# Moving cos and sin from k to v in a fused cosine attention and token mixer, with one transpose of q per head pair, whole-tile stores and a new instruction order

## Chip, cores, metric

One core of one Trainium2 chip. The metric is device microseconds of one execution. The profile's span is about 1.8 us shorter than the time (128.5 against 130.29 us for the profiled run before); spans are compared with spans and times with times. Executions of one kernel differ: a run over 1.5% above the fastest of the same kernel is marked slow, and only fast runs are compared. Clock is the mean share of TensorE's full clock that was granted; "half clock" is a stretch at 0.5.

## The reference, cut

```python
def _attn_ref(q, k, v):                      # 8 batches, 8 heads, 576 tokens, 64 dims
    theta = np.pi / 2.0 * np.arange(S) / S
    def phi(x, c, s):                        # features: relu(x) * cos, relu(x) * sin
        r = np.maximum(x, 0.0)
        return np.concatenate([r * c, r * s], axis=-1)
    q_p, k_p = phi(q, cos_w, sin_w), phi(k, cos_w, sin_w)
    kv = np.einsum('bhsf,bhsd->bhfd', k_p, v)
    z = np.sum(k_p, axis=2)
    num = np.einsum('bhsf,bhfd->bhsd', q_p, kv)
    den = np.einsum('bhsf,bhf->bhs', q_p, z)[..., None] + 1e-06
    return num / den

def _moe_ref(x, w_q, w_k, w_out):            # x: heads side by side, 576 x 512 per batch
    W_tok = (1.0 / np.sqrt(64)) * np.einsum('bsd,btd->bst', x @ w_q, x @ w_k)
    mixed = np.einsum('bst,btd->bsd', W_tok, x)
    return np.maximum(mixed, 0.0) @ w_out
```

The kernel uses that there is no softmax: k'v is 128 features by 64 per head, and the mixer takes (x w_k)' x, which is 64 by 512 per batch.

## The kernel before

An explicit list, `ORDER`, gives every operation, its indices and its engine (`T` TensorE with a bank number, `V` VectorE, `A` ScalarE, `G` GpSimd, `Y` SyncE). Each engine runs its own in order. A head's 576 tokens lie as 64 rows of 9 tokens (`C9`), so two heads stack on 128 partitions, and `H` counts units of four heads (two pairs). The steps of one pair: load (`LD`), relu of k (`RK`), product with cos and sin (`MK`), relu of q, written twice side by side (`DQ`), cast of v (`CV`), k'v and q transposes (`QK`), evacuations of both, that is, copies out of TensorE's output banks (`EK`, `EQ`), num (`NM`), reciprocal (`RC`), scaling (`XN`, the tile `xs`). The mixer: transposes of x (`XT`, `EX`), its products (`WQK`, `TK`, `KX`, `MX`) with evacuations, the output projection (`WO`), output copy (`EO`), store (`ST`).

```python
    def QK(eng, pb, g):                       # per head hh: k'v, then q transposed twice over
        H, i = divmod(g, 2)
        qt, kvp = qk_views(pb)
        for c in range(C9):
            for hh in range(2):
                p0 = hh * 64
                T.matmul(kvp[:, hh, :], kp[H % N_KP][p0:p0 + 64, i, c, :, :],
                         vb[H % N_VB][p0:p0 + 64, i, c, 0:D + 1], start=(c == 0), stop=(c == C9 - 1))
        # ... q transposes of 64 rows, out of the doubled qd
    def EK(eng, pb, g):
        copy(eng, kvs[g % N_KV], qk_views(at["QK", g])[1])

    # MX multiplies for a run of chunks of columns, (0, 5) or (5, 9): mix stays in the order
    # (c, d), so a 128-row output tile holds two runs of 64 tokens, 9 tokens apart
    def ST(eng, pb, b, u, hi):                # one store for each half (hi) of a tile
        ts = (UNITS7 if b == B - 1 else UNITS[b % 2])[u]
        n, _ = unit_of[b, ts[0]]
        bl, c = divmod(2 * (ts[0] + 4 * (b % 2)) + hi, C9)
        row = ((b // 2) * 2 + bl) * S + c
        dst = dataclasses.replace(out, offset=out.offset + row * DM,
            ap=[[C9 * DM, 64], [2 * DM, len(ts)], [1, DM]])
        eng.dma_start(dst, osb[n % N_OSB][64 * hi:64 * hi + 64, 0:len(ts), :])
```

The end of `ORDER`, where 42 stores are shared by two queues, SyncE's (30) and ScalarE's own (12):

```
WO.7.2@T7 ST.6.1.1@A EO.7.1@V WO.7.4@T0 EO.7.2@A WO.7.3@T1 ST.7.1.0@Y ST.7.1.1@A EO.7.4@V
WO.7.0@T2 ST.7.3.0@A EO.7.3@V ST.7.3.1@A ST.7.2.0@Y EO.7.0@A ST.7.2.1@Y ST.7.0.0@A ST.7.0.1@Y
```

## Time and profile before

| | before |
|---|---|
| time, median of 3 (range) | 130.89 us (130.32 to 133.51) |
| span of the profile, clock | 128.5 us, 0.91 |
| last load issued | 99.9 us |
| last of the 32 `xs` scalings ends | 108.6 us |
| last output copy ends | 124.1 us |

The prediction prints the main lines. Three more views matter for what came out. The first is the chain that ended last, its last pieces (start, length, what):

```profile
117.78 2.71 PE banks L413 x12
...
120.51 0.70 DVE osb L187
...
121.23 0.54 ACTq L430
...
121.81 1.60 ACTq L430
...
123.51 0.58 ACT osb L185
```

`ACTq L430` is ScalarE's sequencer issuing stores. It is not counted as busy, but the last output copy, `ACT osb`, is behind it in the same queue: two issues, 2.1 us, on the chain.

The second is the store line looked at by itself: duration of one issue in ns (min/median/max), then first and last start in us.

```profile
L430 SPq DMA_DIRECT2D out_dram<-osb x30: 466/607/1414, 64.6 to 124.1; - x30
...
L430 ACTq DMA_DIRECT2D out_dram<-osb x12: 498/616/1596, 73.8 to 124.1; - x12
```

The third is SyncE's timeline (start, length, what) where the last load is issued:

```profile
94.61 5.25 SPq L430 DMA_DIRECT2D out_dram<-osb  x2
99.91 0.60 SPq L208 DMA_DIRECT2D vf<-in_v_dram  x1
```

Two stores, the second of which waited for an output tile, stand directly ahead of the last load.

### The profile page before, as it was taken

The page shows a single profiled execution, that of the slowest core. Times are in us where ns is not written, and L with a number is a line of the kernel's source. Part 1 is how long each engine was busy: PE and PEld are TensorE (multiplying, and loading weights), DVE is VectorE, ACT ScalarE, POOL GpSimd, SP SyncE. Part 2 cuts the span into 40 slices and gives each one's busy share as a digit, 9 for nine tenths or more (in the row PEclk, how much of TensorE's full clock was granted, in tenths as well). Part 3 has the DMA queues.
Part 4 walks back from the last instruction along what each step waited for, and adds up shares of the span by engine and source line. Part 5 has one row for each costly group of instructions (what it writes and reads, how often), then busy time and mean ns, then how long its engine had stood idle before and what let it go on. Part 6 is the DMA issues. An engine that isn't in the chain of part 4 may idle for free.

```text
span 128.5 us, 5197 instructions
## 1 busy us (share of the span) xinstructions
PE 105.4 (82%) x2198; PEld 69.4 (54%) x2198; DVE 106.2 (83%) x227; ACT 77.5 (60%) x124; POOL 69.4 (54%) x81
## 2 busy tenths in 40 slices
PE   5935594887879979878999969889999999999900
PEld 2314584847667546566676557364576775543400
DVE  3466999987899999999999896999999998774600
ACT  7125443966396698974976758647977655147110
POOL 7009817098969979995078252389949740020000
PEclk9995558655799999999999999999999999999995
DMA  4999999999999999992068999999998799468793
GB/s 133 276 389 406 391 391 390 331 392 388 389 387 392 391 385 391 390 386 103 5 146 319 303 360 363 340 329 403 384 377 309 176 341 248 107 197 278 186 289 100
DMA packets 20711, 39.40 MB, mean 307 GB/s; under 512 B 3280, under 2 KB 3280, under 8 KB 20688
## 3 DMA queue, kind: packets, MB, share of 16 engines
q1 hardware_dynamic: 19152, 36.32, 81.8%
q10 hardware_dynamic: 1536, 2.75, 6.1%
q8 instruction: 17, 0.28, 0.9%
q14 instruction: 6, 0.05, 0.1%
HBM read 29.62 MB, written 9.44 MB: 304 GB/s over the span
## 4 chain that ended last, share of the span: by engine, by line
DVE 31%; PE 30%; POOL 10%; DMA 8%; SPq 7%; issue 6%; ACT 3%; ACTq 2%; POOLq 0%
DVE kp L232 10%; PE banks L413 10%; DVE xs L309 8%; DVE qpt L279 7%; POOL qd L195 5%; PE banks L260 5%; SPq L208 5%; DMA qf<-in_q_dram 5%; PE banks L269 4%; DMA vf<-in_v_dram 4%; PE banks L292 3%; SPq L430 2%; DVE rec L305 2%; PE banks L343 2%; POOL vb L189 2%
## 5 line engine op out<-in xcount | busy, mean ns | idle before, releaser
L195 POOL TENSOR_SCALAR qd<-qf 128x1152 bf16<-128x1152 f32 x32 | 39.1, 1231 | 12.7 <-DMA qf<-in_q_dram 11.6
L413 PE MATMUL banks<-wo_sb,mix 128*128 128x512 bf16 x144 | 36.0, 380 | 0.0
L232 DVE TENSOR_TENSOR kp<-rk,cossin 128x1152 bf16<-128x1152 bf16 x32 | 29.2, 932 | 1.4 <-POOL rk L195 1.3
L185 ACT COPY osb<-banks 128x512 f32<-128x512 f32 x31 | 18.0, 589 | 12.9 <-PE banks L413 8.2
L309 DVE TENSOR_TENSOR xs<-banks,rec 128x640 bf16<-128x640 f32 x32 | 25.4, 808 | 0.3
L279 DVE TENSOR_TENSOR qpt<-banks,cst 128x1152 bf16<-128x1152 bf16 x32 | 23.9, 746 | 1.1 <-PE banks L269 0.8
L401 ACT ACTIVATE mix<-banks 128x640 bf16<-128x640 f32 (+1 forms) x27 | 17.4, 656 | 8.7 <-PE banks L388 8.1
L260 PE MATMUL banks<-vb,kp 64*128 64x65 bf16 x576 | 16.7, 202 | 3.8 <-DVE kp L232 1.8
L413 PEld LDWEIGHTS <-mix 128*128 128x128 bf16 x144 | 12.1, 98 | 12.5 <-issue 1.4
L292 PE MATMUL banks<-kvs,qpt 128*128 128x65 bf16 x320 | 16.2, 203 | 3.1 <-DVE kvs L187 2.2
L269 PE MATMUL banks<-ident,qd 64*128 64x64 bf16 x576 | 16.2, 201 | 2.2 <-POOL qd L195 2.2
L292 PEld LDWEIGHTS <-qpt 128*128 128x128 bf16 x320 | 13.8, 103 | 7.1 <-DVE qpt L279 2.5
L260 PEld LDWEIGHTS <-kp 64*128 64x128 bf16 x576 | 13.6, 100 | 7.2 <-DVE kp L232 2.5
L193 ACT ACTIVATE rk<-kf 128x576 bf16<-128x576 f32 x15 | 10.1, 684 | 9.1 <-DMA kf<-in_k_dram 8.9
L195 POOL TENSOR_SCALAR rk<-kf 128x576 bf16<-128x576 f32 x14 | 11.3, 812 | 6.6 <-DMA kf<-in_k_dram 2.8
L189 POOL TENSOR_SCALAR vb<-vf 128x576 bf16<-128x576 f32 x17 | 12.3, 726 | 4.6 <-DMA vf<-in_v_dram 3.5
L269 PEld LDWEIGHTS <-qd 64*128 64x128 bf16 x576 | 12.9, 102 | 2.4 <-POOL qd L195 2.4
L185 ACT COPY xT<-banks 128x1280 bf16<-128x1280 bf16 x10 | 12.2, 1225 | 2.9 <-PE banks L326 2.9
L185 ACT CAST vb<-vf 128x576 bf16<-128x576 f32 x14 | 9.4, 673 | 4.7 <-DMA vf<-in_v_dram 4.5
L326 PE MATMUL banks<-ident,xs 64*128 64x64 bf16 x320 | 7.8, 196 | 4.2 <-DVE xs L309 4.1
L189 POOL TENSOR_SCALAR wq<-wqk 64x576 bf16<-64x576 bf16 x4 | 2.8, 712 | 14.9 <-DVE wqk L187 7.8
L343 PE MATMUL banks<-xT,wqk_sb 128*128 128x288 bf16 x64 | 10.1, 306 | 0.7 <-DVE xs L309 0.3
(46 smaller groups left out, 112.8 us busy)
## 6 DMA issues: line engine op xcount, KB each, us to landing
kf<-in_k_dram SPq DMA_DIRECT2D x32, 288.0 KB, 6.0
vf<-in_v_dram SPq DMA_DIRECT2D x32, 288.0 KB, 5.9
qf<-in_q_dram SPq DMA_DIRECT2D x32, 288.0 KB, 6.0
out_dram<-osb SPq DMA_DIRECT2D x21, 256.0 KB, 4.4
out_dram<-osb ACTq DMA_DIRECT2D x9, 256.0 KB, 4.3
out_dram<-osb SPq DMA_DIRECT2D x9, 128.0 KB, 3.4
wo_f<-in_moe_w_out_dram SPq DMA_DIRECT2D x1, 1024.0 KB, 8.3
out_dram<-osb ACTq DMA_DIRECT2D x3, 128.0 KB, 4.0
```

The lines of the kernel that those rows point to most:

```text
L185: A.copy(dst, src)
L189: eng.tensor_scalar(dst, src, 1.0, 1.0, op0=ALU.mult, op1=ALU.mult)
L195: eng.tensor_scalar(dst, src, FMAX, 0.0, op0=ALU.min, op1=ALU.max)
L232: eng.tensor_mul(kp[H % N_KP][:, lo:hi], rk[H % N_RK][:, lo:hi].unsqueeze(3).to_broadcast([P, n, C9, 2, D]), cossin.unsqueeze(1).to_broadc ...
L260: T.matmul(kvp[:, hh, :], kp[H % N_KP][p0:p0 + 64, i, c, :, :], vb[H % N_VB][p0:p0 + 64, i, c, 0:D + 1], start=(c == 0), stop=(c == C9 - 1))
L269: T.transpose(qt[:, hh, c * D:(c + 1) * D], src, ident[p0:p0 + 64, p0:p0 + 64])
L279: eng.tensor_mul(qpt[g % N_QPT][:, :, 1:SLOTS, :], qk_views(at["QK", g])[0].rearrange("f h (c d) -> f h c d", c=C9), cst.unsqueeze(1).to_b ...
L292: T.matmul(nv[:, hh, u, :], qpt[g % N_QPT][:, hh, 2 * u:2 * u + 2, :], kvs[g % N_KV][:, hh, :], start=(u == 0), stop=(u == SC - 1 and not ...
L309: eng.tensor_tensor(xs[b % N_XS][:, :, 2 * pr:2 * pr + 2, :].rearrange("p u h d -> p h u d"), num_view(at["NM", g])[:, :, :, 0:D], rec[g % ...
L343: T.matmul(w[:, nh, :], wqk_sb[:, dmc, :], xT[b % N_XT][:, dmc, D + nh * HS:D + (nh + 1) * HS], start=(dmc == 0), stop=(dmc == NDM - 1))
L401: A.activation(dst, src, AF.Relu, scale=scale_moe)
L413: T.matmul(o, mix[b // 2 % N_MIX][:, dmc, base:base + P], wo_sb[:, dmc, :], start=(dmc == 0), stop=(dmc == NDM - 1))
```

## The change

The intent: take work off VectorE, the busiest engine, and make fewer, larger instructions.

1. cos and sin go into v instead of k (`VK`, with a column of cos or sin to give the denominator). k'v is then a 64-row by 64-column product, and four run side by side in quarters of the array.
2. q is no longer written twice. Its transpose is made once per two heads stacked in rows, and `EQ` reads it for cos and for sin.
3. One ScalarE copy evacuates k'v of four heads (262 columns), in place of two VectorE ones of 130.
4. x is transposed in full 128x128 tiles (`XT_FULL`).
5. `MX` takes strided columns and `EMX` writes mix in token order, so an output tile is 128 consecutive tokens and goes out in one store: 21 stores on SyncE.
6. A new `ORDER`, which also moves evacuations from VectorE to ScalarE, k relus to GpSimd, and all stores to SyncE. The numbers of buffers change with it, among them the output tiles (6 to 8).

```diff
-            eng.tensor_mul(kp[...], rk[...].unsqueeze(3).to_broadcast([P, n, C9, 2, D]), cossin...)
+    def VK(eng, pb, H, j):
+        eng.tensor_mul(vv[H % N_VV][:, j, :, :, 0:D],
+            vb[H % N_VB][:, j].unsqueeze(2).to_broadcast([P, C9, 2, D]), cossin)
...
+    def KV(eng, pb, H):
+        kvp = bank2(pb, 0, 4 * NV, FP32)
+        for c in range(C9):
+            for j in range(2):
+                for r in range(2):
+                    T.matmul(kvp[64 * j:64 * j + 64, r, :], rk[H % N_RK][64 * r:64 * r + 64, j, c, :],
+                             vv[H % N_VV][64 * r:64 * r + 64, j, c].rearrange("p w d -> p (w d)")[:, 0:NV],
+                             start=(c == 0), stop=(c == C9 - 1))
...
     def NM(eng, pb, g):
-        for hh in range(2):
-            for u in range(SC):
-                T.matmul(nv[:, hh, u, :], qpt[g % N_QPT][:, hh, 2 * u:2 * u + 2, :],
-                         kvs[g % N_KV][:, hh, :], ...)
+        for u in range(SC):
+            for w in range(2):
+                for j in range(2):
+                    p0 = 64 * j
+                    T.matmul(nv[:, j, u, :], qpt[g % N_QPT][p0:p0 + 64, w, 2 * u:2 * u + 2, :],
+                             kvs[H % N_KV][p0:p0 + 64, r, w, 0:D + 1], ...)
...
     def XT(eng, pb, H):
+                if full:
+                    T.transpose(xv[:, i, u, :], x, ident)
+                    continue
...
     def MX(eng, pb, b, j):
-        c0, c1 = ((0, 5), (5, 9))[nh]
+                     w.rearrange("p (c d) -> p c d", c=C9)[:, :, h * TH:(h + 1) * TH],
     def EMX(eng, pb, b, j):
+            :, :, i, o:o + NT].rearrange("p r (d c) -> p r d c", c=C9)
...
-    def ST(eng, pb, b, u, hi):
-            ap=[[C9 * DM, 64], [2 * DM, len(ts)], [1, DM]])
-        eng.dma_start(dst, osb[n % N_OSB][64 * hi:64 * hi + 64, 0:len(ts), :])
+    def ST(eng, pb, b, u):
+        row = (b // 2) * 2 * S + (ts[0] + 4 * (b % 2)) * P
+            out, offset=out.offset + row * DM, ap=[[DM, P], [P * DM, len(ts)], [1, DM]])
+        eng.dma_start(dst, osb[n % N_OSB][:, 0:len(ts), :])
```

## The prediction

> **What bounds the kernel now.** I read the page first, then the busy time by stretches, the waits of the SP queue, and the groups by form.
>
> The page, engines and slices:
>
> ```profile
> PE 105.4 (82%) x2198; PEld 69.4 (54%) x2198; DVE 106.2 (83%) x227; ACT 77.5 (60%) x124; POOL 69.4 (54%) x81
> ...
> DVE  3466999987899999999999896999999998774600
> ...
> PEclk9995558655799999999999999999999999999995
> DMA  4999999999999999992068999999998799468793
> ```
>
> DVE is at 9 from 18 us to about 105 us. DMA is full up to 57 us, has a hole at 60 to 67 us, and is full again to 93 us. PE runs at half clock for about 20 us in the first 34 us.
>
> The stretches (length, then PE, PEld, DVE, ACT, POOL busy, clock, DMA share, GB/s):
>
> ```profile
> 36.00:60.00 24.00, 20.91 (x526) 14.16 (x525) 23.55 (x48) 18.87 (x31) 21.37 (x22) 1.00 0.99 367
> 60.00:68.00 8.00, 7.83 (x210) 5.67 (x203) 7.90 (x18) 6.50 (x11) 3.00 (x3) 1.00 0.29 64
> 68.00:100.00 32.00, 29.44 (x687) 19.40 (x686) 29.79 (x66) 22.77 (x38) 20.25 (x23) 1.00 0.98 350
> ...
> 100.00:128.50 28.50, 21.89 (x288) 11.90 (x283) 17.05 (x33) 10.71 (x19) 3.97 (x6) 0.95 0.74 216
> ```
>
> From 36 to 100 us DVE works 61.2 of 64 us, 96%. PE shows 91%, but that counts each matmul's latency: a 128x65 num matmul lasts 203 ns and starts every 29 to 34 ns, so PE has more room than it shows. The DMA hole is an effect of slow compute:
>
> ```profile
> SPq L208 <- ACT rk L193: 8.6, 1, 8.6
> ```
>
> One load of k waits 8.6 us for a raw buffer, because the relu that frees it stands behind a late ACT queue. The last load is issued at 99.9 us. The work before it is DVE-bound; the 28.6 us after it are a tail of mixer work, in which PE is full from 110 to 120 us.
>
> The groups that the change touches:
>
> ```profile
> L195 POOL TENSOR_SCALAR qd<-qf 128x1152 bf16<-128x1152 f32 x32 | 39.1, 1231 | 12.7 <-DMA qf<-in_q_dram 11.6 <-PE banks L269 0.3
> L232 DVE TENSOR_TENSOR kp<-rk,cossin 128x1152 bf16<-128x1152 bf16 x32 | 29.2, 932 | 1.4 <-POOL rk L195 1.3
> L279 DVE TENSOR_TENSOR qpt<-banks,cst 128x1152 bf16<-128x1152 bf16 x32 | 23.9, 746 | 1.1 <-PE banks L269 0.8
> L185 ACT COPY osb<-banks 128x512 f32<-128x512 f32 x31 | 18.0, 589 | 12.9 <-PE banks L413 8.2 <-issue 3.3 <-DMA qf<-in_q_dram 0.9
> L187 DVE CAST kvs<-banks 128x130 bf16<-128x130 f32 x32 | 8.7, 281 | 1.1 <-ACT xT L185 1.0
> L187 DVE COPY xT<-banks 128x1280 bf16<-128x1280 bf16 x6 | 4.8, 815 | 0.0
> L187 DVE COPY osb<-banks 128x512 f32<-128x512 f32 x5 | 3.5, 692 | 2.8 <-PE banks L413 2.8
> ```
>
> **What the Trainium skill says.** (1) "SBUF — State Buffer", Who interferes with whom: a Vector tensor_tensor with both inputs in SBUF contends with GpSimd for an exclusive port pair. The trace agrees: the 13 kp products with under 20% of their time beside POOL average 0.68 us, the 12 with over 80% average 1.07 us. (2) "VectorE: DVE Perf Modes", Why PSUM operands drop a tier: a PSUM operand still allows the 2x bf16 mode, fp32 stays at 1x. It agrees: qpt from PSUM takes 0.746 us for 1152 elements, about the 0.75 us median of kp, so the new broadcast form should too. (3) "TensorEngine Tiling (Array Packing)", Key Properties: a change of tiling mode drains TensorE, and tiles run independently. It agrees: a 512-column matmul is followed by the same mode after 216 ns, by another after 312 ns, so a drain is about 0.1 us. (4) The same page, Gotcha 2: column tiling excludes fast weight load. The trace fits: the 64-column weight loads of kx take 110 ns, the 128-column ones 95 to 98 ns; two column tiles still load 3 to 4 ns apart, so four 64x64 tiles should overlap. The trace before has no 64x64 tiles, so that step is inferred.
>
> **The change, part by part.** Durations are the group means. The two programs' engine queues give the counts.
>
> DVE. The k product becomes the v product (cos and sin go into v): 32 products of 1152 elements either way, 29.2 us or a little less, as POOL has less work. The q product (32 x 0.746), num scaling (32 x 0.81) and reciprocals stay. Removed: 32 kvs casts, 8.7; five output copies, 3.5; three of six xT copies, 2.4; four of five mix relus, 2.9; three k relus, 1.7; one v cast, one wqk, two kx copies, 2.4; one more wkj copy costs 0.3. Sum -21.3 us. 106.2 becomes about 85.
>
> ACT. Added: 16 kvs copies of 262 columns at about 0.375 (kx of 256 takes 0.370), 6.0; 14 q relus at 0.68, 9.6; five output copies, 2.9; three xT copies, 3.7; four mix relus, 2.6; kx, wqk and cst, 1.9. Removed: eight k relus, 5.5; two v casts, 1.3; three wq copies, 2.0; one wkj, 0.4. Sum +17.5: 77.5 becomes about 95. ACT's 12 store issues go to SP, some 0.6 us each that were never counted as busy, so ACT's real load rises by about 10.
>
> POOL. 32 q relus of 1152 elements (39.1) become 18 of 576 at about 0.75 (13.5), since q is no longer duplicated. Added: 11 k relus at 0.81, 8.9; three v casts, 2.2; three wq copies, 2.1; six small copies of cos, about 1. Sum -11: 69.4 becomes about 58.
>
> PE, at full clock, from start-to-start times in the trace. k'v: 32 x 0.285 = 9.1 before; after, 16 x 9 groups of four tiles, 131 columns at 2.4 columns/ns = 55 ns, with 0.05 for fill: 16 x 0.55 = 8.8. q transposes: 32 x 0.26 = 8.3, then 16 x 0.26 = 4.2. num: 32 x 0.31 = 9.9, then 32 x 20 x 14.5 ns = 9.3. xs transposes: 16 x 0.29 = 4.6, then full tiles 160 x 56 ns = 9.0. Mode changes, counted from the order: 80 to 97, +1.7 us. The output projection (36 x 0.86 = 31) and the mixer stay. Sum: -0.3 -4.1 -0.6 +4.4 +1.7 = about +1. PE is neutral at about 90 us.
>
> DMA. The same 39.4 MB, at the 390 GB/s of the full slices 101 us. 42 stores of 64 rows become 21 of 128, so SP has 119 issues and ACT none. Eight output buffers instead of six allow stores to come late: only six stand ahead of the last load, 14 or more before.
>
> **The sum.** I cut the time at the last load's issue. Before: DVE has about 88 us of work ahead of it; start at 8 us plus 88/0.96 gives 99.7, measured 99.9. After: work ahead of it, total minus the operations listed after it, is DVE 85-15 = 70, ACT 95-24 = 71, PE 90-28 = 62 plus some 10 for half clock; DMA 29.6 MB plus 2.6 of stores less 2 in flight, 30.2/0.39 = 77. With starts at 8, 4, 5 and 2 us the floors are 78, 75, 77 and 79: four resources nearly level. No resource is then at 96% as DVE was; I allow 8 us for waits in turn, so 87 us. The tail: 28 us of PE work remain (19 output tiles alone 16.3, before only 14), ACT 24, and the last copy and store need 2 to 3: about 31, against 28.6. Span 118; the measured time before is about 2 us over its profile span: 120. I choose 119.5.
>
> **The rivals.** *ACT becomes the bound.* It evacuates kvs, xT, wqk, kx, mix and every output tile in one in-order queue, and now also holds kvs on the way from k'v to num. For it: the 8.6 us wait above shows one late ACT instruction stopping loads. Against: 95 of 118 us is 80%. If ACT loses a further 6 us, the time is about 126. *Column tiling serializes.* If the 64x64 weight loads go one after another at 27 ns (an estimate: the 13 ns by which kx loads exceed the fast ones is half of a 64-column load at 2.4 columns/ns), each k'v takes 0.97 us, PE gains 7 us, and the end is about 123. Against: the 3 ns start distance of kx pairs. *DMA hides the gain.* If stores pile up at the end, 15 stores of at most 0.5 MB stand after the last load, under 7 MB, 18 us in 31: not a bound unless bunched, +2 us. *Better than balanced:* if loads stay full to the last, the end is near 112 to 114.
>
> **Range and chances.** DVE's 21 us are real removals from the binding engine, and no floor is over 80 us up to the last load, so slower needs two rivals at once. Range 113.5 to 126. Faster by over 2% (under 128.3) 0.88, within 2% 0.09, slower 0.03.
>
> **What would show it.** DVE busy 82 to 88 us with the v product at 0.7 to 0.95 us; ACT 92 to 98; POOL 55 to 62; k'v about 0.55 us per 36 matmuls at full clock; no DMA hole over 3 us before the last load; last load issued at 83 to 91 us; tail 29 to 33 us. It is wrong if the v product falls out of the 2x mode (over 1.2 us each, +15 us of DVE), if the transposed read of the mix copies slows them from about 0.65 us (31 on ACT; 0.2 us more each is +6 us), if PE's half clock lasts beyond 40 us, or if stores on SP hold up loads.

## The result, and the profile after

After: median 123.97 us (123.52 to 125.53), before in the same session 130.92 us. The ratio is 0.9472, with an interval of 0.9417 to 0.9527. A ratio is the mean time of one kernel's fast runs over that of the other's fast runs of the same rounds, so not quite the ratio of the medians quoted. One run after (125.53) was slow and is not used; the profile: span 122.0, clock 0.93.

The page after, engines and slices:

```profile
PE 104.4 (86%) x2056; PEld 67.0 (55%) x2070; DVE 87.2 (71%) x174; ACT 92.0 (75%) x155; POOL 58.7 (48%) x90
...
PE   5934885999686999998969997999999999999970
...
DVE  2054899859999798999999995987798779412000
...
DMA  4999999999999999998996299999999896244595
```

VectorE lost 19 us of work and is at 9 in fewer slices. PE stands at 9 from the slice at 76 us to 116 us. There is still a gap in DMA at 64 to 70 us.

The stretches after (length, then PE, PEld, DVE, ACT, POOL busy, clock, DMA share, GB/s):

```profile
36.00:60.00 24.00, 21.98 (x493) 13.82 (x495) 22.26 (x41) 20.43 (x37) 18.55 (x23) 1.00 1.00 359
60.00:68.00 8.00, 6.92 (x178) 5.06 (x179) 7.64 (x17) 7.62 (x13) 3.30 (x4) 1.00 0.77 276
68.00:100.00 32.00, 30.69 (x669) 20.02 (x673) 26.88 (x53) 26.69 (x49) 17.36 (x24) 1.00 0.96 350
100.00:122.00 22.00, 17.95 (x184) 9.30 (x186) 5.67 (x14) 14.14 (x25) 1.33 (x2) 1.00 0.57 211
```

Before, VectorE was busy 29.79 of the 32 us from 68 us; now it is 26.88, and PE is the highest with 30.69. The groups that answer to those of before:

```profile
L219 DVE TENSOR_TENSOR vv<-vb,cossin 128x1152 bf16<-128x1152 bf16 x32 | 27.8, 893 | 7.1 <-ACT vb L180 6.1
L257 DVE TENSOR_TENSOR qpt<-banks,cst 128x1152 bf16<-128x1152 bf16 x32 | 22.9, 747 | 4.5 <-PE banks L250 4.2
...
L180 ACT COPY osb<-banks 128x512 f32<-128x512 f32 x36 | 20.9, 591 | 2.4 <-PE banks L403 1.7
...
L190 POOL TENSOR_SCALAR qd<-qf 128x576 bf16<-128x576 f32 x18 | 13.4, 745 | 14.6 <-DMA qf<-in_q_dram 13.9
...
L180 ACT CAST kvs<-banks 128x262 bf16<-128x262 f32 x16 | 6.1, 381 | 6.5 <-PE banks L236 6.3
```

Each of these operations costs about what was foreseen. VectorE now idles (7.1 us in front of `vv`) for casts of v on ScalarE. The wait of SyncE behind the DMA gap (us in total, times, longest) is one v cast on ScalarE, where before it was a k relu on ScalarE:

```profile
SPq L197 <- ACT vb L180: 5.6, 1, 5.6
```

The end of the chain after, and the store line:

```profile
113.03 4.64 PE banks L403 x21
...
117.72 0.61 PE banks L403 x2
...
118.36 0.59 ACT osb L180
```

```profile
L418 SPq DMA_DIRECT2D out_dram<-osb x21: 332/394/2037, 59.1 to 119.0; - x21
```

The last copy now starts when its matmuls end (0.04 us after them); before, it started 1.3 us after them. That is half of what was gained behind the last matmul. Most of the other half is the last store itself: from issue to landing it took 3.3 us before and takes 2.2 now. A store of 128 rows holds its queue for 0.39 us in the median, one of 64 rows held it for 0.61. Summed, issuing stores takes 10.5 us of SyncE; before it took 22.2 us of SyncE and 8.3 us of ScalarE.

**Where the 6.5 us of span went.** Both kernels make 32 scalings `xs` of the same shape, so the trace can be cut at the end of the ninth, of the last, and at the end of the last matmul. The table holds all kernels, from their profiles. The last column is the state of that profile; rows marked slow are for reading only. Each figure is rounded by itself.

| kernel | start to 9th scaling | 9th to last | to last matmul | to the end | span | state |
|---|---|---|---|---|---|---|
| before | 42.9 | 65.7 | 13.6 | 6.3 | 128.5 | fast |
| after | 39.3 | 65.1 | 13.9 | 3.7 | 122.0 | fast |
| e3_before_newmix | 41.7 | 65.8 | 13.6 | 3.7 | 124.8 | fast |
| e1_ek_dve | 38.9 | 65.6 | 13.9 | 3.7 | 122.1 | fast |
| e3_dve_heavy | 44.3 | 73.8 | 13.9 | 3.7 | 135.6 | fast |
| e2_xt_twice | 40.2 | 68.8 | 15.0 | 3.7 | 127.7 | fast |
| e1_cv_pool | 36.6 | 66.1 | 13.9 | 3.7 | 120.4 | fast |
| e2_warm | 37.4 | 65.9 | 13.9 | 3.7 | 121.0 | fast |
| e3_best | 38.5 | 64.6 | 13.9 | 3.7 | 120.8 | fast |
| e1_old_mix | 36.7 | 68.9 | 14.0 | 6.7 | 126.3 | slow |
| e2_store_split | 38.9 | 67.7 | 14.4 | 6.5 | 127.4 | slow |
| e2_before_act | 43.0 | 69.8 | 14.0 | 6.6 | 133.4 | slow |
| e1_xt_half | 39.9 | 65.8 | 13.8 | 3.7 | 123.2 | slow |
| e3_best_half | 40.8 | 64.6 | 13.8 | 3.7 | 122.9 | slow |

From before to after: -3.6, -0.6, +0.3, -2.6. VectorE's busy time in these stretches went from 34.8 to 28.1 us, from 62.5 to 57.3 and from 8.9 to 1.9. So only 5.2 of its 19 us went out of the long middle, where it was 95% busy, and that stretch hardly got shorter.

### The profile page after: what moved, and what is told of

It is laid out like the page before. It is cut to its first block, busy times and chain, and to the rows that moved or that the text cites. A ratio compares the mean times of both kernels' runs of the same rounds, so it can differ in the third digit from the quotient of the medians.

```text
span 122.0 us, 4895 instructions
## 1 busy us (share of the span) xinstructions
PE 104.4 (86%) x2056; PEld 67.0 (55%) x2070; DVE 87.2 (71%) x174; ACT 92.0 (75%) x155; POOL 58.7 (48%) x90
## 4 chain that ended last, share of the span: by engine, by line
PE 49%; DVE 26%; DMA 15%; issue 4%; ACT 2%; SPq 1%; POOL 1%; ACTq 0%; DVEq 0%
PE banks L403 20%; DVE vv L219 10%; DVE xs L292 7%; DVE qpt L257 6%; DMA qf<-in_q_dram 6%; PE banks L236 5%; PE banks L332 5%; DMA kf<-in_k_dram 5%; PE banks L271 5%; PE banks L379 4%; DMA vf<-in_v_dram 4%; PE banks L360 3%; PE banks L310 3%; PE banks L250 2%; DVE rec L287 2%
## 5 line engine op out<-in xcount | busy, mean ns | idle before, releaser
L219 DVE TENSOR_TENSOR vv<-vb,cossin 128x1152 bf16<-128x1152 bf16 x32 | 27.8, 893 | 7.1 <-ACT vb L180 6.1
L391 ACT ACTIVATE mix<-banks 128x576 bf16<-128x576 f32 x31 | 19.5, 655 | 2.3 <-PE banks L379 1.0
L190 POOL TENSOR_SCALAR qd<-qf 128x576 bf16<-128x576 f32 x18 | 13.4, 745 | 14.6 <-DMA qf<-in_q_dram 13.9
L271 PE MATMUL banks<-kvs,qpt 64*128 64x65 bf16 x640 | 15.3, 198 | 1.0 <-ACT kvs L180 0.9
L271 PEld LDWEIGHTS <-qpt 64*128 64x128 bf16 x640 | 13.1, 99 | 4.6 <-issue 2.7
L236 PE MATMUL banks<-vv,rk 64*64 64x131 bf16 x576 | 14.3, 237 | 1.4 <-DVE vv L219 0.6
L236 PEld LDWEIGHTS <-rk 64*64 64x64 bf16 x576 | 10.8, 116 | 4.6 <-issue 2.9
L188 ACT ACTIVATE qd<-qf 128x576 bf16<-128x576 f32 x14 | 9.6, 686 | 4.2 <-DMA qf<-in_q_dram 4.0
L310 PE MATMUL banks<-ident,xs 128*128 128x128 bf16 x160 | 12.3, 231 | 0.0
L310 PEld LDWEIGHTS <-xs 128*128 128x128 bf16 x160 | 10.3, 104 | 2.3 <-DVE xs L292 0.3
```

The costliest lines, as they stand in the source:

```text
L190: eng.tensor_scalar(dst, src, FMAX, 0.0, op0=ALU.min, op1=ALU.max)
L219: eng.tensor_mul(vv[H % N_VV][:, j, :, :, 0:D], vb[H % N_VB][:, j].unsqueeze(2).to_broadcast([P, C9, 2, D]), cossin)
L236: T.matmul(kvp[64 * j:64 * j + 64, r, :], rk[H % N_RK][64 * r:64 * r + 64, j, c, :], vv[H % N_VV][64 * r:64 * r + 64, j, c].rearrange("p w ...
L271: T.matmul(nv[:, j, u, :], qpt[g % N_QPT][p0:p0 + 64, w, 2 * u:2 * u + 2, :], kvs[H % N_KV][p0:p0 + 64, r, w, 0:D + 1], start=(u == 0 and ...
L310: T.transpose(xv[:, i, u, :], x, ident)
L391: A.activation(dst, src, AF.Relu, scale=scale_moe)
```

## The experiments

Three theories stood at the outset: the gain comes from VectorE's relief and its balance with ScalarE; TensorE has become the limit of the second half; loads, and the gap in DMA, set the end. The rival to all three: the form of the stores (halves or whole tiles) does it. Every kernel here gave the right result. "Before" was run again with each set; its medians there were 132.02, 132.09 and 131.97 us, with 17 of those 25 runs slow, so the ratios have wide intervals. Where it helps, the text compares fast runs with fast runs of "after" (mean of three, 123.82). "After" was not run again with the sets, and the third set (e3) ran on another chip than the first two; the mean of the fast runs of "before" moved between 130.06 and 131.35 us from set to set. So differences to "after" of about 1 us are not told from noise.

### Stores

**e1_old_mix**: the mixer products, mix and stores of before, in the new order.

```diff
-                     w.rearrange("p (c d) -> p c d", c=C9)[:, :, h * TH:(h + 1) * TH],
+            w = (wqk[b % N_WQK][0:64, D + c0 * D:D + c1 * D] if r == 0 else wq2[...])
-        eng.dma_start(dst, osb[n % N_OSB][:, 0:len(ts), :])
+        for hi in range(2):
+            ST1(eng, pb, b, u, hi)          # 64 rows, 9 tokens apart, as before
```

> The changed kernel, with mix, its relu copies and the stores as in the kernel before (chunks of 5 and 4 columns of 64, stores of 64 rows each, two for one, all on SP: 42 instead of 21). Theories 1 to 3 all expect the same time within 1 us, since the copies cost the same 0.655 us on average and the stores are not the bound. The rival that whole-tile stores carry part of the gain expects 2 to 4 us slower, with loads held up behind stores on SP.

Measured: median 127.17 us, ratio 0.9736 (0.9549 to 0.9923). The fast runs, 125.76, 127.0 and 127.34, average 2.9 us over the fast runs of after. So undoing only this part loses about two fifths of the gain: the rival is right here. The profile was slow; its last column in the table, 6.7 us, is taken up below.

**e2_store_split**: is it the order of mix or the store's form? Token order stays, each store goes out as two of 64 rows.

```diff
-        eng.dma_start(dst, osb[n % N_OSB][:, 0:len(ts), :])
+        for hi in range(2):
+            dh = dataclasses.replace(out, offset=out.offset + (row + 64 * hi) * DM,
+                                     ap=[[DM, 64], [P * DM, len(ts)], [1, DM]])
+            eng.dma_start(dh, osb[n % N_OSB][64 * hi:64 * hi + 64, 0:len(ts), :])
```

> The changed kernel, with each store of 128 rows issued as two of 64 rows, both on SP, mix still in token order: 42 stores instead of 21. The run with the old mix and the old stores was 3 us slower; its last output copy ended 1.3 us later than in the changed kernel, but its end 4.3 us later. If the number of stores on SP does that: 2 to 4 us slower than the changed kernel, the last store issued about 2.5 us or more after the last output copy. If the old row order of mix does it: within 1 us.

Measured: 127.35 us, ratio 0.9691 (0.9598 to 0.9784); fast runs 127.14, 127.22 and 127.49, 3.5 us over after. The form of the store alone gives all that e1_old_mix gave. Its store line, as above:

```profile
L421 SPq DMA_DIRECT2D out_dram<-osb x42: 487/610/1878, 59.1 to 124.0; - x42
```

610 ns for 64 consecutive rows, 607 for 64 rows that lie 9 apart: their spacing makes no difference here, and 128 rows took 394. These are medians; single issues lasted up to 1.9 us here and 2.0 us in after. SyncE's timeline from 112 us to the end, of after and then of the split:

```profile
112.01 7.29 SPq L418 DMA_DIRECT2D out_dram<-osb  x6
```

```profile
112.10 12.49 SPq L421 DMA_DIRECT2D out_dram<-osb  x14
```

The lengths run from the first start to the last end, waits for output tiles included. With whole tiles the last store starts 0.03 us after the last copy (118.94 us). With halves, eight issues stand almost without a gap from 118.86 us on, and four of them start after the last copy (121.54 us), the last at 124.0. That is the end column: 6.3 to 6.7 us from the last matmul to the end in each of the four kernels with half-tile stores, 3.7 in each of the ten with whole tiles, whatever else they do, in fast and slow profiles alike.

**e3_before_newmix**: the same part put alone into the kernel before. The two halves of mix take 36 and 28 of the 64 rows, since with 32 and 32 an output tile of the old order would read columns not yet written. There are 14 stores on SyncE and 7 on ScalarE.

```diff
-        c0, c1 = ((0, 5), (5, 9))[nh]
+        d0, d1 = ((0, 36), (36, 64))[h]
+                     w.rearrange("p (c d) -> p c d", c=C9)[:, :, d0:d1],
-            ap=[[C9 * DM, 64], [2 * DM, len(ts)], [1, DM]])
+            ap=[[DM, P], [P * DM, len(ts)], [1, DM]])
-WO.7.0@T2 ST.7.3.0@A EO.7.3@V ST.7.3.1@A ST.7.2.0@Y EO.7.0@A ST.7.2.1@Y ST.7.0.0@A ST.7.0.1@Y
+WO.7.0@T2  EO.7.3@V ST.7.3@A  EO.7.0@A ST.7.2@Y  ST.7.0@Y
```

> The kernel before, with only the mix in token order (halves of 36 and 28 of the 64 steps, so that its own order of operations stays valid) and stores of whole tiles: 21 instead of 42 issues, each at the place of the second of its pair, on the queue of that one. Splitting the stores in the changed kernel cost 3.3 us. If that part of the gain stands alone: 2 to 4 us faster than before. If it is only worth something with the new order (because before, ScalarE's queue took 12 of the stores): within 1 us of before.

Measured: 126.24 us, six fast runs from 126.03 to 126.81; ratio 0.9711 (0.9611 to 0.9811), against only two fast runs of before. About 3.7 us gained by the fast means (126.34 against 130.06), and all six runs are below all eleven of before. No work was taken off any engine:

```profile
PE 105.3 (84%) x2198; PEld 69.0 (55%) x2198; DVE 106.8 (86%) x227; ACT 77.9 (62%) x124; POOL 70.3 (56%) x81
```

VectorE is as busy as before, and the middle took 65.8 us as before. Of the 3.7 us of span, 2.6 lie behind the last matmul. Here the chain ends as in after: no `ACTq` stands before the last copy, although ScalarE still issues seven stores.

```profile
116.60 4.44 PE banks L414 x20
...
121.06 0.59 ACT osb L185
```

The other 1.2 us lie before the ninth scaling at 41.7 us, while the first store is issued at 64.6: no store can have made them. Half clock lasted 17.1 us of the first 40 here and 20.5 before, which may be the reason; it was not tested in this kernel.

This run also answers for the last load. SyncE's timeline around it:

```profile
88.92 0.33 SPq L208 DMA_DIRECT2D vf<-in_v_dram  x1
98.15 3.89 SPq L429 DMA_DIRECT2D out_dram<-osb  x4
```

The last load goes out at 88.9 us instead of 99.9. Six stores stand ahead of it, 16 before. VectorE's work is unchanged, so the amount of it was not what held the last load; and 11 us of earlier loading moved the last scaling by 1.2 us, no more than the lead it had from the start.

### VectorE

**e1_ek_dve**: the 16 k'v evacuations go back to VectorE, `EK.n@A` to `EK.n@V` for all n.

> The changed kernel, with all 16 kvs copies put back on VectorE: VectorE +16 x 0.39 = 6 us of work (87 to 93), ScalarE 6 us less (92 to 86). Theory 1: within 1.5 us of the changed kernel. Theory 3 with VectorE as the bound: 3 to 6 us slower; with ScalarE as the bound: 2 to 5 us faster.

```profile
PE 103.8 (85%) x2070; PEld 66.4 (54%) x2070; DVE 91.0 (74%) x190; ACT 87.5 (72%) x139; POOL 57.0 (47%) x90
```

Measured: 123.77 us (123.57 to 124.79), ratio 0.9528 (0.9364 to 0.9693): no change. 3.8 us more on VectorE cost nothing, and 4.5 us less on ScalarE gained nothing. Unless the two cancel, neither is the limit.

**e2_before_act**: relief of VectorE, paid for on ScalarE, in the old order. In the kernel before, 45 evacuations go from `@V` to `@A`: 32 of k'v, five output copies, five of mix, one of x w_q and two of kx. No position in the list changes.

> The kernel before, with the kvs copies and the five output, five mix, two kx and one wqk copies moved from VectorE to ScalarE, nothing else: VectorE about 17 us less (106 to 89), ScalarE about 17 more (77 to 94), nearly the balance of the changed kernel. If the gain is the relief of VectorE: 3 to 7 us faster than before. If it takes the new order, or the gain is TensorE's or the stores': within 2 us of before, or slower, as ScalarE's queue then comes late for an order that was not made for it.

```profile
PE 107.0 (80%) x2198; PEld 69.7 (52%) x2198; DVE 93.7 (70%) x182; ACT 89.3 (67%) x169; POOL 69.1 (52%) x81
```

Measured: 132.87 us, ratio 1.0096 (0.9975 to 1.0216); fast runs 132.06, 132.23 and 133.5. VectorE fell by 12.5 us, ScalarE rose by 11.8, and no time was gained. The profile was slow; its busy times serve only to show that the work did move, and where: 1.8 us went before the ninth scaling, 3.4 in the middle, 7.3 after it. In the old order this exchange is worth nothing, which does not exclude that relief is worth something in an order made for it, or without the load on ScalarE.

**e3_dve_heavy**: how much can VectorE take in the new order? `EK` back on VectorE, and the denominators computed twice.

```diff
-            eng.tensor_scalar_add(rec[g % 4], den, EPS)
-            eng.reciprocal(rec[g % 4], rec[g % 4])
+            for _ in range(2):
+                eng.tensor_scalar_add(rec[g % 4], den, EPS)
+                eng.reciprocal(rec[g % 4], rec[g % 4])
```

> The changed kernel, with the kvs copies back on VectorE and every denominator and reciprocal computed twice: VectorE +6 and +12 us of work, so 100 to 104 us busy, nearly the 106 of the kernel before; ScalarE 6 less. If the relief of VectorE carries the rest of the gain: 3 to 6 us slower than the changed kernel. If TensorE and the stores decide it: less than 2 us slower.

```profile
PE 110.9 (82%) x2070; PEld 70.1 (52%) x2070; DVE 102.5 (76%) x254; ACT 88.1 (65%) x139; POOL 55.1 (41%) x90
```

Measured: 136.51 us, six fast runs from 135.73 to 137.46, ratio 1.0507 (1.0381 to 1.0634): 12.5 us more than after for 15.3 us of work. That is more than either forecast, and slower than the kernel before with less work on VectorE than that one had (106.2). So the new order bears 3.8 us more on VectorE (e1_ek_dve), but not this. Whether the load does it isn't shown: the second reciprocal also lies in the chain from num to scaling, so it is latency as well, and in the middle VectorE was 92% busy (68.2 of 73.8 us), less than in the kernel before.

### TensorE

**e1_xt_half**: x transposed in halves of 64 rows again, `XT_FULL = ()`. The estimate from start-to-start times, 4.3 us less for TensorE, is in the expectation.

> The changed kernel, with the xs transposes back in 64-row halves, all else the same. It takes about 160 x 56 - 320 x 14.5 ns = 4.3 us of TensorE work out, about half of it after 68 us. Theory 1 (from about 70 us to the end TensorE is the bound: it has no idle time over 0.2 us there): 1.5 to 3 us faster than the changed kernel, ratio to the kernel before about 0.93. Theory 2 (the loads are the bound up to 90 us, and the tail follows them): within 0.7 us of the changed kernel. Theory 3 (VectorE or ScalarE is the bound): within 0.7 us, or slower, as the xT copies then write with strides.

Measured: 124.73 us (fast 122.81 and 124.5), ratio 0.9502 (0.9161 to 0.9843): no gain that shows, a miss for the theory that TensorE limits the second half, with only two fast runs 1.7 us apart. Mode changes rose from 40 to 47 from TensorE's 90th operation on, which takes back about 0.7 us at 0.1 us each; that is not enough to explain it.

**e2_xt_twice**: the opposite; every full transpose is issued twice, 160 more of 56 ns, 9 us.

```diff
                 if full:
                     T.transpose(xv[:, i, u, :], x, ident)
+                    T.transpose(xv[:, i, u, :], x, ident)
```

> The changed kernel, with each full xs transpose issued twice (same result): TensorE work +160 x 56 ns = 9 us, about half of it after 68 us. If TensorE is the bound of the second half: 4 to 8 us slower than the changed kernel (128 to 132 us). If something else is (loads, VectorE, ScalarE, or the length of the chain from load to output): less than 2 us slower, as TensorE would fill its idle time.

The stretches from 60 to 100 us, columns as above, first of after and then of this kernel:

```profile
60.00:100.00 40.00, 37.61 (x846) 25.08 (x852) 34.51 (x69) 34.31 (x61) 20.67 (x27) 1.00 0.92 335
```

```profile
60.00:100.00 40.00, 39.23 (x863) 27.01 (x861) 33.10 (x65) 33.27 (x58) 20.38 (x27) 1.00 0.83 306
```

Measured: 129.32 us (127.69 to 129.6), ratio 0.982 (0.9709 to 0.9932). 9 us of TensorE cost 5.3 us by the medians, 3.7 of them in the middle. TensorE goes to 98% busy there and VectorE does less per microsecond. So TensorE is within a few microseconds of being the limit; more work there shows, less (e1_xt_half) does not. As with the reciprocals, the added transposes also lengthen the chain from scaling to output.

### Loads

**e1_cv_pool**: the cast that made the load wait 5.6 us, `CV.11.0`, moves from ScalarE to GpSimd and earlier in the list.

```diff
-EMX.2.3@A CV.10.0@G EQ.20@V CV.10.1@A ...
+EMX.2.3@A CV.10.0@G CV.11.0@G EQ.20@V CV.10.1@A ...
-CV.11.0@A XN.18@V CV.11.1@G ...
+XN.18@V CV.11.1@G ...
```

> The changed kernel, with one v cast (pair 11, first half) moved from ScalarE, where it stood in the queue until 67.7 us, to an earlier place on GpSimd. A load of v waited 5.6 us for it, and with it all later loads (the DMA hole at 62 to 68 us). Theory 1 (TensorE bound late): the hole goes, the last load is issued 3 to 5 us earlier, and the end moves by less than 1.5 us. Theory 2 (loads bound): the end moves by 3 to 5 us with the loads. Theory 3 (VectorE or ScalarE): less than 1 us.

The DMA slices; the gap at 64 to 70 us is gone, and loading ends earlier (the gap at 90 us comes after the last load):

```profile
DMA  3999999999899999997999999999970796244595
```

Measured: 123.25 us (fast 122.2, 123.06, 123.43), ratio 0.9444 (0.9287 to 0.96). The last load goes out at 84.0 us instead of 89.7. The last scaling ends 1.6 us earlier, but the ninth, at 36.6 instead of 39.3 us and long before the edit acts, had already 2.7 us of lead. From there on it is 1.1 us slower. 5.7 us of earlier loads bought nothing that shows: the gap in DMA was not on the path.

### The clock at the start

**e2_warm**: 26 warm-up matmuls instead of 14, and 19 dummy matmuls of 512 columns in an unused bank among the first operations (`WU.3@T7` and the like).

> The changed kernel, with 12 more warm-up matmuls before the first work and 19 dummy matmuls between the first operations on TensorE, into a bank that is not yet in use, so that its clock is not halved between 9.8 and 26.8 us. The chain of waits has about 6 us of TensorE pieces in that window. If the half clock delays everything behind it: 1.5 to 3 us faster, the xs of batch 2 (ninth num scaling) at 37 us instead of 39. If the loads set the pace there: within 0.7 us.

Measured: 122.84 us (122.02 to 123.53), ratio 0.9352 (0.9238 to 0.9465), 1.0 us below after's fast mean. TensorE ran at full clock until the end (mean 0.993). The ninth scaling ended at 37.4 us instead of 39.3, though e1_cv_pool, with 13.7 us of half clock, had 36.6. So all of the half clock at the start is worth at most one or two microseconds, no more than the start differs between runs: after, e1_cv_pool and e2_store_split have the same instructions up to there and took 39.3, 36.6 and 38.9 us.

### A better version

**e3_best** joins e2_warm and e1_cv_pool; **e3_best_half** adds `XT_FULL = ()`.

> The changed kernel with the warm-up between the first operations and the early v cast of pair 11 on GpSimd together. Each alone gave about 1 us or less. If TensorE is the bound from 68 us on, the earlier loads help little and the sum is about 1 to 2 us faster than the changed kernel (122 to 123 us); if loads were the other half of the cause, 3 us or more.

> The run before with the xs transposes in 64-row halves besides: TensorE 4.3 us less work, about 2 us of it after 68 us, less 0.7 for seven more mode changes there. If TensorE is the bound: 1 to 2 us faster than that run (120.5 to 122). In the first trial of the halves alone the profiled run had a stretch of half clock at 39 us; with the warm-up that is expected not to decide. If the full transposes were free: within 0.5 us.

Measured: e3_best 123.04 us (fast 121.22, 122.53, 123.01), ratio 0.94 (0.9172 to 0.9627); e3_best_half 124.87 us (fast 122.55, 123.4), ratio 0.9455 (0.9144 to 0.9767). e3_best is about 1 us below after by the medians (1.6 by the fast runs), with intervals that overlap, so this is not shown to be faster. Nor is it shown to differ from e2_warm. Half transposes again gained nothing: the middle took 64.6 us in both profiles (that of the halves a slow one).

## Why the prediction was right, and where it was not

The time, 123.97 us, is inside 113.5 to 126 and 4.5 us over the predicted 119.5; "faster" was right. Step by step:

- **The work of each engine: right.** DVE 87.2 (82 to 88), ACT 92.0 (92 to 98, at its edge), POOL 58.7 (55 to 62), the v product 893 ns (0.7 to 0.95 us).
- **k'v in 64x64 tiles: right.** 36 matmuls start within 0.50 us, and the next operation 0.65 us after the first, mode change included (0.55 foreseen). The rival in which column tiles load one after another (0.97) is out. "PE is neutral" is not contradicted: 105.4 and 104.4 us busy, though busy time counts latency too.
- **The last load (83 to 91) and the tail (29 to 33): in range**, at 89.7 and 32.3 us. Span 122.0 instead of 118: 2.7 us at the first, 1.3 at the second.
- **"No DMA hole over 3 us": wrong.** A cast late on ScalarE made one load wait 5.6 us, the very mechanism the ACT rival gave. e1_cv_pool shows no gain without it.
- **"DVE's 21 us are real removals from the binding engine": the step that failed.** The removals are real, 19 us, but a high share of busy time was taken for a bound. In the middle, where VectorE was 95% busy, its busy time fell by 5.2 us and the stretch by 0.6. After the last scaling it fell by 7.0 us and the stretch grew by 0.3. Moving 12.5 us from VectorE to ScalarE in the old order gave nothing, putting 3.8 back in the new one cost nothing. A share of 96% says that an engine is hardly ever idle; it does not say that the others would be faster without it. TensorE was near (29.44 of 32 us before, 30.69 after); that it took the place is not shown.
- **"I cut the time at the last load's issue": the cut was wrong.** Start at 8 us plus 88/0.96 gave 99.7 against 99.9 measured, and e3_before_newmix shows that this agreement proved nothing. Two stores stood directly ahead of that load, and whole-tile stores moved it to 88.9 us with VectorE's work unchanged. The last load isn't on the path anyway: 11 us (e3_before_newmix) and 5.7 us (e1_cv_pool) earlier gained no more than each run's lead at the ninth scaling.
- **Stores: missed.** The prediction counted the 0.6 us per issue, but only as hidden load on ScalarE, and looked at bytes ("18 us in 31: not a bound"). What counted was the queue. A whole tile takes 0.39 us to issue and a half 0.61, so 42 issues on one queue outlast the copies, and with two queues two of them stood before the last copy. Three experiments show 2.9 to 3.7 us by the fast runs; by their profiles, two of them slow, 2.6 to 3.0 us lie behind the last matmul.
- **Two readings were off,** without weight in the sum. VectorE was not at 9 all the way from 18 to 105 us: the slices show 7 and 8 from 26 to 35 us, 8 at 71 and 6 at 77. And the k products beside GpSimd: the trace gives 12 with under 20% beside it, 0.74 us on average, and 11 with over 80%, 1.16 us, not 0.68 and 1.07; the shortest of all is 0.70. The direction stands.

So the prediction came out right in time partly by luck: a relief that was overrated stood in for a store cost that was overlooked. By the profiles, 2.6 of the 6.5 us are behind the last matmul, and that part is shown to come from the stores. 3.6 us, the larger part, are before the ninth scaling and have no cause shown; 0.3 are in between.

**What stays open.** The 3.6 us at the start have no isolated cause. The new order is ahead there in every profile but that of e3_dve_heavy (36.6 to 40.2 us in the other fast ones, 41.7 and 42.9 with the old order), while the loads are issued at nearly the same times up to 50 us. The half clock explains one or two at most. VectorE's relief is a rival that was not tested there: its busy time fell by 6.7 us in this stretch, and e2_before_act took out only 1.8. e3_dve_heavy put 4.2 back and was 5.0 later, but with more latency and with 23.1 us of half clock against 17.1. The single copy of q, the lighter GpSimd and the order were not tested apart either. What limits the middle after the change isn't settled either: 3.8 us more on VectorE do not show, TensorE shows extra work but no saving, and earlier loads do not show. That fits several engines within a few microseconds of one another, joined by in-order queues, but it is not shown. The profiles of e1_old_mix and e2_store_split suggest 3 us more in the middle with half stores; they were slow, so this is not claimed.

## What to carry to other kernels

Before crediting a change with work taken off the busiest engine, cut the trace at markers that both kernels share and ask which stretch should shrink; then test the relief alone, by moving the work and by putting it back. Look at the queues and not only at the engines: a store's issue time stands in no busy column, and at the end of a kernel it decides when the last copy runs and when the last byte leaves. Store whole 128-row tiles. Whether stores must also leave the queue of the engine that makes the last copies was not tested alone: e3_before_newmix kept seven whole-tile stores on ScalarE and had the same 3.7 us behind the last matmul.

## What the Trainium skill lacked or had wrong

- "DMA: Bandwidth & Descriptors", Issuing engines are not separate DMA queues, calls the time that a sequencer needs to initiate a DMA "usually small relative to the DMA itself", and gives no figure by number of rows. Here a 64-row store held its queue for 0.61 us in the median and a 128-row one for only 0.39; the runs do not say why. The 42 half stores held queues for 30.6 us in all, and the form was worth 2.9 to 3.7 us of 130. The page's advice in Rules for kernel authors, one 128-partition transfer instead of two halves, agrees with the runs; its reason there is shared DMA engines, and the runs add the queue.
- "VectorE: DVE Perf Modes", The perf-mode tier table, lists a tensor_tensor with any PSUM operand at 1x. Here such a product took 747 ns for 1152 bf16 elements per partition, as long as the product from SBUF of the same size does in the median (756 ns; its mean is 893); the page's own section Why PSUM operands drop a tier (2x stays possible) is right.
- "TensorE: Matmul & The Clock Gate", Part 4: PE-mode transpose, gives about 275 to 390 ns for a 128x128 transpose. Here one lasts 231 ns on average but the next starts 56 ns later, so in a row they cost a quarter of what the duration says; Part 4 has no time from start to start.
- "TensorEngine Tiling (Array Packing)", Key Properties, says that a change of mode drains the engine but not what that costs: about 0.1 us here (312 against 216 ns to the next start). Nor does the page have a time for 64x64 tiles: groups of four products of 131 columns start 56 to 62 ns apart (82 from the first to the second), 36 products in 0.50 us.
